# An S4 layer with a feed-forward block: eight of sixteen input rows get their shift after the move, four residual rows are loaded early, and the planned order is new

## The chip, the core and the metric

The kernel runs on one core of a Trainium2 chip. The metric is the device time of one execution in microseconds; the time of the kernel before is the median of three runs. The engines are named as in the profile: PE is TensorE's matmuls and PEld its weight loads, DVE is VectorE, ACT is ScalarE, POOL is GpSimd, SP issues most of the DMAs.

## What is computed

The input is 2048 tokens of 512 channels. A conditioning vector gives six vectors by a small product (`mod = silu(c) @ w_mod`). The first half is a layer norm with scale and shift, an S4 convolution over the tokens (by Fourier transforms of length 4096, its kernel K built from complex exponentials), a gate and a residual; the second half is a layer norm, a dense layer of 1792, a squared ReLU, a dense layer back, a gate and a residual.

```python
h = layernorm(x) * (1 + ca) + sa
K = einsum("dn,dnl,dn->dl", C, exp(dt * A * l), dt * B).real
y = irfft(rfft(h) * rfft(K)) + h * Dskip          # along the tokens
x = x + ga * y
h = layernorm(x) * (1 + cb) + sb
x = x + gb * (relu(h @ w1 + b1) ** 2 @ w2 + b2)
```

## The kernel before, in words

**Rows.** The input stands in memory as 16 blocks `xt[s]` of 128 x 512, the "rows". For each row the kernel takes mean and variance (L681, L682, with a power on GpSimd at L685 and L686, four rows at a time), subtracts the mean and multiplies by the gain `g1` (L729, VectorE, in place), and then moves the row into another layout with sixteen small matmuls on TensorE (L742). The matrix of the move, `sel`, is the identity scaled by the row's reciprocal deviation (L737, ScalarE). The shift `s4` of the modulation, the same for all rows, is put into the bank first, by a matmul of two constants (`pick`, `shift`, L739) into which the move accumulates. ScalarE copies the bank into `xj` (L745). The banks `ps` are three, shared by nearly everything before the feed-forward part.

**The S4 part.** Channels are worked in eight chunks. For chunk c, letters A to H are the transform of the input (stage 1 L789, stage 2 L799, copies on ScalarE L791 and L824), the digits 0 to 7 are the exchange of its halves by DMA (L834), letters a to h are the product with the kernel's transform (L949, VectorE) and the sums that go back (L957, copies L963). Stage 1 needs all sixteen rows. The kernel itself is made in 32 units u between these pieces: phases (L892, GpSimd), sines (L902 to L904, ScalarE), amplitudes (L914, L918, GpSimd), their products (L928 to L931, VectorE), a small matmul (L938) and its stage 1. The units need the parameters of their chunk (`parameters`, L595 to L664: the four first chunks at once, the other four as piece p, which itself is split over VectorE, ScalarE and GpSimd) and the exponentials (piece x, L883). Piece r is a row, l the later half of the modulation, w a part of the load of w1.

**What follows.** `inverse` (L1123) goes back to tokens, two row blocks at a time (L1131), and adds the residual `xt`: rows 0 to 3 on VectorE from a buffer `cd4` (L1140), the others on GpSimd (L1145). Then come layer norm, transposes (L1168) and the two dense layers in three float32r products per product (L1245, L1272 to L1274), which fill TensorE to the end.

**What sets the order.** `LOADS` is the order of the first loads on SP: x a row, p and P the two halves of the parameters, G, C and S three 1 MB blocks of `w_mod` (gate, scale, shift), t and e tables of the transforms, k Dskip. `ORDER` says which pieces are written between which units. That written order gives the dependencies and the ring of banks; then `keep_order` (L181) plans the sequence on each engine, with a cost for every instruction (`weight`, L121). `SPAN` is how far ahead a more urgent group may be taken before an earlier one, and `PASSES` how often the plan is made anew from its own latest starts. Matmuls in `in_turn` keep their written order; the inverse of rows 0 to 3 was among them. `paced_load` lets a load wait until the one before the last has landed. Engines work through their queues in order, so an instruction that waits holds all behind it.

## Time and profile before

| | |
|---|---|
| runs | 605.31 us median (601.77 to 606.57) |
| profiled execution | 605.23 us, of it 603.4 in the span |
| PE, PEld busy | 569.5, 494.1 us |
| DVE, ACT, POOL busy | 438.4, 421.5, 464.0 us |
| rows (first L739 to end of the last L745) | 24.6 to 49.5 us |
| stage 1 begins (L789) | 49.5 us |
| inverse begins (L1131) | 272.8 us |
| HBM read, written | 46.74, 4.19 MB |

Durations are those of one profiled execution. In a row of the timeline the first number is the start, the second the length (of a whole run of instructions where it ends in a count, x32); in brackets stands the idle time of that engine before it and what ended it. In a row of the groups stand the count, the busy time in us, the mean ns of one instruction, and the idle time before. The records of one fp32 matmul are two. "Issue" is time in which an engine waited for nothing that the profile shows.

### The profile page before, as it was taken

How to read it: one execution, taken by the hardware profiler on the slowest of the kernel's cores; microseconds unless marked ns; L12 is line 12 of the kernel's file. 1: busy time of each engine (PE TensorE's matmuls, PEld its weight loads, DVE VectorE, ACT ScalarE, POOL GpSimd, SP SyncE). 2: the span in 40 equal slices, each digit the busy share in tenths (PEclk: the TensorE clock that was granted, in tenths of full speed). 3: DMA queues.
4: the chain of work that ended last, by engine and by line, in shares of the span. 5: the costliest groups of instructions: out<-in, count | busy, mean ns of one | idle time of the engine just before them, and what ended most of it. 6: DMA issues, size and time to landing. Idle time of an engine off the chain costs nothing.

```text
span 603.4 us, 21634 instructions
## 1 busy us (share of the span) xinstructions
PE 569.5 (94%) x9396; PEld 494.1 (82%) x9396; DVE 438.4 (73%) x714; ACT 421.5 (70%) x788; POOL 464.0 (77%) x383
## 2 busy tenths in 40 slices
PE   1898999999999999998989999999999999998996
PEld 1667988999999998997778888888887888887885
DVE  7796688899798799746888945459859744547833
ACT  4997999998999879442879555546957555654440
POOL 5599999999999799160668998926689688892544
PEclk9999999999999999998999999999999999999999
DMA  8962033302130234274351332015354343201432
GB/s 306 398 193 72 5 73 74 64 12 44 34 74 4 51 104 100 52 195 145 103 147 57 105 104 89 22 45 176 107 153 127 112 119 102 70 18 35 158 88 86
DMA packets 45982, 60.70 MB, mean 101 GB/s; under 512 B 5184, under 2 KB 26816, under 8 KB 45760
## 3 DMA queue, kind: packets, MB, share of 16 engines
q1 hardware_dynamic: 45456, 59.20, 33.5%
q8 instruction: 73, 1.20, 0.9%
q10 hardware_dynamic: 432, 0.14, 0.1%
q14 instruction: 21, 0.17, 0.1%
HBM read 46.74 MB, written 4.19 MB: 84 GB/s over the span
## 4 chain that ended last, share of the span: by engine, by line
PE 69%; ACT 8%; POOL 7%; DVE 6%; issue 5%; DMA 4%; DVEq 0%; POOLq 0%; ACTq 0%; SPq 0%
PE ac L1245 9%; PE ps L1245 8%; PE ps L957 8%; PE ps L799 8%; PE ps L789 6%; PE ac L1274 4%; PE ac L1272 4%; PE ac L1273 4%; PE kg L938 4%; DMA xy<-w 4%; PE kg L1245 3%; PE ac L1131 3%; PE ps L1274 2%; PE ps L1272 2%; PE ps L1273 2%
## 5 line engine op out<-in xcount | busy, mean ns | idle before, releaser
L1214 POOL TENSOR_TENSOR w2r<-xy,w2r 128x512 fp32r<-128x512 f32 x56 | 80.1, 1431 | 53.9 <-ACT w2r L1213 53.7
L799 PE MATMUL ps<-xy,t_sb 128*64 128x64 f32 x2048 | 67.3, 223 | 1.0 <-issue 0.7
L799 PEld LDWEIGHTS ps<-xy,t_sb 128*64 128x64 f32 x2048 | 64.2, 138 | 3.1 <-issue 0.9
L957 PE MATMUL ps<-e_sb,xy 128*64 128x128 f32 (+2 forms) x1152 | 65.3, 267 | 1.1 <-issue 0.8
L957 PEld LDWEIGHTS ps<-e_sb,xy 128*64 128x64 f32 x1152 | 59.5, 140 | 2.6 <-issue 1.4
L1213 ACT CAST w2r<-xy 128x512 fp32r<-128x512 f32 x56 | 34.8, 624 | 27.1 <-PE ac L1274 12.7
L918 POOL TENSOR_TENSOR rtl<-tables 128x1024 f32<-128x1024 f32 x22 | 43.2, 1964 | 0.0
L1272 PE MATMUL ac<-w2r,r 128*128 128x512 f32 x110 | 42.8, 389 | 0.0
L1273 PE MATMUL ac<-w2r,r 128*128 128x512 f32 x110 | 42.8, 389 | 0.0
L1274 PE MATMUL ac<-w2r,r 128*128 128x512 f32 x110 | 42.8, 389 | 0.0
L791 ACT COPY xy<-ps 128x512 f32<-128x512 f32 x64 | 36.6, 590 | 8.7 <-PE ps L789 8.4
L1245 PE MATMUL ac<-tt,k1t 128*128 128x512 f32 x168 | 40.6, 390 | 1.5 <-DVE xy L1378 1.5
L949 DVE TENSOR_TENSOR xy<-ps,xy 128x512 f32<-128x512 f32 x64 | 40.1, 685 | 2.1 <-PE ps L799 1.1
L1245 PEld LDWEIGHTS ac<-tt,k1t 128*128 128x128 f32 x168 | 31.5, 188 | 8.4 <-DVE xy L1378 1.9
L1145 POOL TENSOR_TENSOR big<-big,xy 128x512 f32<-128x512 f32 x12 | 16.1, 1357 | 26.3 <-ACT big L1142 26.2
L1237 POOL TENSOR_TENSOR k1t<-xy,k1t 128x1024 fp32r<-128x1024 f32 x14 | 33.7, 2407 | 3.3 <-ACT k1t L1235 3.1
L892 POOL TENSOR_TENSOR rtl<-lo,big 128x1024 int32<-128x1024 int32 x16 | 34.3, 2143 | 2.4 <-ACT tg L904 2.3
L963 DVE COPY big<-ps 128x256 f32<-128x256 f32 (+1 forms) x66 | 24.7, 411 | 15.7 <-PE ps L957 15.5
L892 POOL TENSOR_TENSOR llph<-lo,big 128x1024 int32<-128x1024 int32 x16 | 34.5, 2157 | 0.8 <-ACT tg L904 0.8
L1272 PE MATMUL ps<-w2r,r 128*128 128x512 f32 (+1 forms) x88 | 34.7, 394 | 0.0
L789 PE MATMUL ps<-d_sb,big 128*64 128x128 f32 x512 | 32.1, 274 | 2.4 <-ACT xy L791 1.7
L1274 PE MATMUL ps<-w2r,r 128*128 128x512 f32 (+1 forms) x88 | 34.0, 386 | 0.0
(297 smaller groups left out, 1693.8 us busy)
## 6 DMA issues: line engine op xcount, KB each, us to landing
xy<-w SPq DMA_DIRECT2D x91, 256.0 KB, 2.8
xy<-xt SPq DMA_DIRECT2D x32, 256.0 KB, 4.5
xy<-xy SPq DMA_DIRECT2D x32, 256.0 KB, 3.6
xy<-w_mod SPq DMA_DIRECT2D x6, 1024.0 KB, 9.0
out_dram<-p SPq DMA_DIRECT2D x15, 256.0 KB, 2.0
t_sb<-c_t SPq DMA_DIRECT2D x1, 2048.0 KB, 11.5
i2c<-c_i SPq DMA_DIRECT2D x4, 512.0 KB, 4.2
big<-prm SPq DMA_DIRECT2D x2, 768.0 KB, 6.2
```

What stands on the lines that cost most here:

```text
L789: nc.tensor.matmul(ps[64 * r : 64 * r + 64, 128 * i : 128 * i + 128], src[:, i], d1_sb[:, r], start=True, stop=True)
L791: copy(dst[:, o // 4], ps.rearrange("p (t m) -> p m t", t=4))
L799: nc.tensor.matmul(ps[64 * r : 64 * r + 64, 64 * i : 64 * i + 64].rearrange("p (h q t) -> p q h t", h=2, t=2), t2_sb[:, 8 * g + i, r], src ...
L892: nc.gpsimd.tensor_tensor(ph.rearrange("p d r (a b) -> p (d r) a b", a=4), bc(low_phase[:, us].rearrange("p d r b -> p (d r) b"), 2, 4), b ...
L918: nc.gpsimd.tensor_mul(am[:, 0, :, 32:96].rearrange("p d (v x) -> p d v x", v=2), bc(et[:, 256 + 8 * d0 : 384 + 8 * d0].rearrange("p (y a) ...
L949: nc.vector.tensor_mul(product_piece(y, g), ps, piece(x, g))
L957: nc.tensor.matmul(ps[64 * m : 64 * m + 64], pairs(y)[:, g, i // 2, 64 * m : 64 * m + 64, i % 2], e1_sb[:, h].rearrange("p (r j) -> p r j" ...
L1214: nc.gpsimd.tensor_sub(to[:, 1], wst, to[:, 0].bitcast(F32))
L1245: nc.tensor.matmul(ps[:, cols], x, y, start=(i == 0 and not onto), stop=(i == 5), skip_group_check=onto)
L1272: pe.append(nc.tensor.matmul(bank_, r2l[:, ms], hi_[:, cols], start=(f == begin), stop=False))
L1273: pe.append(nc.tensor.matmul(bank_, r2h[:, ms], lo_[:, cols], start=False, stop=False))
L1274: pe.append(nc.tensor.matmul(bank_, r2h[:, ms], hi_[:, cols], start=False, stop=(f == end_)))
```

## The change

*The shift of a row.* A string `EVAC` gives each row a way out of its bank. Rows with a (4 to 8, 10, 13, 14) are as before. For v (2, 3, 11, 12, 15) the matmul of `pick` and `shift` is left out, and VectorE adds `s4` as it takes the bank over. For g (0, 1, 9) it is left out too, ScalarE copies the bank, and GpSimd then adds `s4` in place.

*The residual's first rows.* A new piece y, as soon as the last amplitude has been issued, loads xt[0] to xt[3] into four parts of `p1`, which lies where the second exponential table was; before, they went into a spectrum buffer together with rows 4 to 7, behind the table of the inverse. The inverse of rows 0 to 3 is no longer in `in_turn`.

*Order.* `LOADS`, `ORDER`, `PASSES` and `SPAN` are new, and the planner's cost knows a transpose. The line numbers of the changed kernel are larger: L739 is L744, L742 is L747, L745 is L754 (the adds are L752 and L756), L729 is L732, L892 is L904, L1131 is L1152.

```diff
+EVAC = "ggvvaaaaagavvaav"
-LOADS = "pxxxxxxxxGCSxxxxxxxkPtxe"
+LOADS = "xxxxpxGxxCPxSxxxxketxxxx"
-PASSES, SPAN = 7, 400
+PASSES, SPAN = 10, 150
-    "rrrrrrrrrrxxrrrrrrBCCBpACCBCBAABCCBAB.AAAAC..lB.0aaaa1.a.Daa.x.DabbbbDEDEE.b.2Ebb.bD.DcDccccEDc.E.Fc"
+    "rrrrrrrrrrrrrrrrBCBCCBAAAxCBABABCCxC..ApAABC.l0.aaBaa1..aDaaD..abbbbEDEEbbE.E.b.D.Db2DDcxccDc3..EcEc"
...
+            if ins.is_transpose:
+                return 88, 88 + 130
...
-            nc.tensor.matmul(ps.rearrange("p (g d) -> p g d", g=4), pick, bc(shift, 1, 4), start=True, stop=False)
+            late = EVAC[s] != "a"
+            if not late:
+                nc.tensor.matmul(ps.rearrange("p (g d) -> p g d", g=4), pick, bc(shift, 1, 4), start=True, stop=False)
             for g in range(4):
                 for q in range(4):
                     nc.tensor.matmul(
                         ps[32 * q : 32 * q + 32, 128 * g : 128 * g + 128], sel[:, g // 2, 32 * (g % 2) : 32 * (g % 2) + 32],
-                        row[:, 128 * q : 128 * q + 128], start=False, stop=(g == 3))
-            moved.append(nc.scalar.copy(xj[:, :, 4 * s : 4 * s + 4], ps.rearrange("p (g d) -> p d g", g=4)))
+                        row[:, 128 * q : 128 * q + 128], start=late, stop=late or g == 3)
+            to, of = xj[:, :, 4 * s : 4 * s + 4], ps.rearrange("p (g d) -> p d g", g=4)
+            if EVAC[s] == "v":
+                nc.vector.tensor_add(to, of, bc(s4, 2, 4))
+            else:
+                nc.scalar.copy(to, of)
+            if EVAC[s] == "g":
+                nc.gpsimd.tensor_add(to, to, bc(s4, 2, 4))
+            moved.append(s)
...
+    def early_rows():
+        assert amped[-1] == NU - 1
+        late.append(held(kp, "k01", "p1", [P, 7, 512]))
+        for s in range(4):
+            paced_load(late[0][:, 3 + s], xt[s])
+        yield
...
-    xts = [cs_[s] if s < 4 else ds_[s % 4] for s in range(16)]
-    for s in range(8):
+    xts = [ds_[s % 4] for s in range(16)]
+    for s in range(4, 8):
         paced_load(xts[s], xt[s])
...
-    cd4 = runs(spectra[3]).rearrange("p (s q c d) -> p s q c d", s=4, q=4, c=NC)
+    cd4 = p1[:, 3:7].rearrange("p s (q c d) -> p s q c d", q=4, c=NC)
...
-        if s0 < 4:
-            in_turn.update(whole)
```

How the plan moves instructions is seen at three places. First, ScalarE's queue at the start of the rows, before: `tables` are the exponentials, `tg0` the angle of the first parameters, `big1` the moved rows.

```order
L635 ACT_TABLE_LOAD
L635 ACTIVATE tg0_171<-halfpi_70 128x1
L636 ACTIVATE tg0_171<-tg0_171 128x256
L719 CAST shift_319<-s4_318 128x128
L883 ACT_TABLE_LOAD
L883 ACTIVATE tables1_338<-big0_86 128x2x64 x16
L745 COPY big1_87<-ps1_163 128x128x4
```

And now:

```order
L639 ACTIVATE tg0_171<-tg0_171 128x256
L740 ACTIVATE big0_86<-ident_66,mv1_74 128x2x64
L895 ACT_TABLE_LOAD
L895 ACTIVATE tables0_337<-big0_86 128x64 x8
L648 ACT_TABLE_LOAD
L648 ACTIVATE big0_86<-big0_86 128x4x64
L649 ACTIVATE big0_86<-big0_86 128x4x64
L650 ACTIVATE big0_86<-big0_86,halfpi_70 128x4x64
L722 CAST shift_319<-s4_318 128x128
L895 ACT_TABLE_LOAD
L895 ACTIVATE tables1_338<-big0_86 128x2x64 x8
L754 COPY big1_87<-ps1_163 128x128x4
```

The sine of the first parameters (L648 to L650), with a table load of its own, has come ahead of the first copy of a row; a batch of exponentials has gone behind the arctangent (L639), and eight of the wide ones behind the first copies.

Second, VectorE's queue at the same place, before; `ps0` holds the product that becomes `s4`, `xy0` are rows 0 to 3, `xy2` rows 8 to 11:

```order
L681 BN_STATS st1_76<-xy2_96 128x6
L715 TENSOR_TENSOR s4_318<-ps0_162,gs4_316 128x128
L681 BN_STATS st2_77<-xy2_96 128x6
L720 SCALAR_TENSOR_TENSOR shift_319<-shift_319,small_71,s4_318 128x128
L681 BN_STATS st3_78<-xy2_96 128x6
L682 BN_AGGR mv1_74<-st0_75 128x2
L682 BN_AGGR mv1_74<-st1_76 128x2
L729 SCALAR_TENSOR_TENSOR xy0_94<-xy0_94,mv1_74,kg0_320 128x512 x4
```

And now:

```order
L642 SCALAR_TENSOR_TENSOR tg0_171<-tg0_171,big0_86 128x256
L643 SCALAR_TENSOR_TENSOR tg0_171<-tg0_171,big0_86 128x256
L644 SCALAR_TENSOR_TENSOR tg0_171<-tg0_171,big0_86 128x256
L645 TENSOR_SCALAR big0_86<-tg0_171 128x4x64
L732 SCALAR_TENSOR_TENSOR xy0_94<-xy0_94,mv1_74,kg0_320 128x512 x3
L684 BN_STATS st0_75<-xy2_96 128x6
L718 TENSOR_TENSOR s4_318<-ps0_162,gs4_316 128x128
```

Four steps of the angle stand ahead of the first rows, and `s4` is read behind three rows instead of ahead of all.

Third, SP's queue near the end of the S4 part, before:

```order
L1318 DMA lo_341<-b2 128x512
L669 DMA xy0_94<-xy4_98 64x1024 x4
L669 DMA raw1_3665<-w1 128x4x128
L669 DMA i2c_4586<-c_i2 128x1024 x4
L669 DMA xy4_98<-xt 128x512 x4
L669 DMA xy0_94<-xt 128x512 x4
```

And now:

```order
L1337 DMA lo_341<-b2 128x512
L672 DMA xy6_100<-xy2_96 64x1024 x4
L672 DMA raw1_3803<-w1 128x4x128
L672 DMA p1_4562<-xt 128x512 x4
L672 DMA i2c_4586<-c_i2 128x1024 x4
L672 DMA xy3_97<-xt 128x512 x4
```

Four loads of the residual have moved from behind the inverse's table `i2c` to ahead of it, into `p1`.

More of the change, by code (lines that the diff above doesn't have):

```diff
@@ L44 @@
 EXP_PART = 8
-PASSES, SPAN = 7, 400
+PASSES, SPAN = 10, 150
 EXPS = [(0, 1), (1, 1), (2, 2), (4, 2), (6, 2)]
 ORDER = (
-    "rrrrrrrrrrxxrrrrrrBCCBpACCBCBAABCCBAB.AAAAC..lB.0aaaa1.a.Daa.x.DabbbbDEDEE.b.2Ebb.bD.DcDccccEDc.E.Fc"
-    "3EFc.E.ddddGd.Fd.GxFd4.F.dGeeeeF..FGGFHeGeGe5..wHeffGHfff.w.f.H.HffH6ggHgw.g.g.H.g7ghhhghw"
+    "rrrrrrrrrrrrrrrrBCBCCBAAAxCBABABCCxC..ApAABC.l0.aaBaa1..aDaaD..abbbbEDEEbbE.E.b.D.Db2DDcxccDc3..EcEc"
+    "..cEFcFdFdddGdGFd..FdF..4GdeeGee..xFFeGe.e.5GGHeffHGfffHwf.H.f..Hw6fHHggHgg....gggw7hhhhwyg"
 ).split(".")
@@ L1032, in load_pieces @@
             yield
-    work["w"] = load_pieces()
+    late = []
+    def early_rows():
[4 more added lines that the diff above has]
+        yield
+    work["w"], work["y"] = load_pieces(), early_rows()
     next(work["x"])
@@ L1094, in tile_adaln_ssm_ffn @@
     w2r = held(kp, "k00", "w2r", [P, 3, 2, 512], FR)
-    p1 = held(kp, "k01", "p1", [P, 7, 512])
+    p1 = late[0]
     for _ in last:
```

## The prediction

> **What bounds the kernel now.** I read the page first, then busy time by stage, then the timeline of the first 60 us, where the change sits.
>
> ```profile
> PE 569.5 (94%) x9396; PEld 494.1 (82%) x9396; DVE 438.4 (73%) x714; ACT 421.5 (70%) x788; POOL 464.0 (77%) x383
> ```
>
> TensorE is busy for 569.5 of 603.4 us, so 34 us of idle is all that ordering can win; work taken off TensorE comes on top. By stage:
>
> ```profile
> 0.00:50.00 50.00, 33.57 (x648) 24.47 (x650) 41.26 (x109) 40.01 (x133) 35.74 (x58) 1.00 0.76 271
> ...
> 49.00:267.00 218.00, 211.97 (x6122) 201.68 (x6122) 179.43 (x294) 188.96 (x293) 197.29 (x144) 1.00 0.26 61
> ...
> 100.00:160.00 60.00, 59.51 (x1684) 56.98 (x1682) 51.09 (x85) 55.56 (x92) 59.53 (x45) 1.00 0.18 39
> ...
> 270.00:275.00 5.00, 3.84 (x147) 3.36 (x143) 1.38 (x4) 0.00 (x0) 0.00 (x0) 1.00 0.46 147
> 275.00:280.00 5.00, 4.65 (x171) 3.88 (x175) 3.48 (x11) 0.85 (x3) 0.00 (x0) 0.70 0.48 151
> ...
> 320.00:603.00 283.00, 276.93 (x1240) 228.63 (x1238) 179.34 (x217) 161.19 (x279) 209.83 (x167) 1.00 0.31 94
> ```
>
> The columns are the length, then PE, PEld, DVE, ACT and POOL busy, the granted clock, the DMA share and GB/s. Half of all idle, 16.4 us, lies ahead of 50 us. From 49 to 267 us TensorE idles 6.0 us, and GpSimd beside it is as full (59.53 of 60 from 100 to 160 us): a stage with two bounds. From 320 us on TensorE runs matmuls that the change does not touch; I cost that stage at nothing. The row stage itself:
>
> ```profile
> 24.61 0.50 PE L739 MATMUL ps<-shift,pick 128*128 128x512 f32 x1 [0.29 <-DVE shift L720]
> ...
> 26.08 1.08 PE L742 MATMUL ps<-xy,big 128*32 128x128 f32 x32 [0.98 <-DVE xy L729]
> ...
> 28.53 0.51 PE L739 MATMUL ps<-shift,pick 128*128 128x512 f32 x1
> ...
> 28.96 1.08 PE L742 MATMUL ps<-xy,big 128*32 128x128 f32 x32
> ...
> 29.97 0.50 PE L739 MATMUL ps<-shift,pick 128*128 128x512 f32 x1
> ```
>
> A row takes 29.97 - 28.53 = 1.44 us of TensorE, of which the shift's matmul takes 28.96 - 28.53 = 0.43 and the move 1.01. Thirteen rows from 29.97 give 48.7, and so it ends:
>
> ```profile
> 48.87 0.59 ACT L745 COPY big<-ps 128x512 f32<-128x512 f32 x1 [0.85 <-PE ps L742]
> ...
> 49.51 2.84 PE L789 MATMUL ps<-d_sb,big 128*64 128x128 f32 x48 [0.70 <-ACT big L745]
> ```
>
> From row 3 on, TensorE alone sets the pace of this stage.
>
> **The change part by part.** Removed: eight shift matmuls, 8 x 0.43 = 3.4 us of TensorE. That is a gain only if nothing else in the row stage ends later, so I follow each queue. The rows for it:
>
> ```profile
> 17.77 1.28 ACT L737 ACTIVATE big<-ident,mv 128x128 f32<-128x128 f32 x4 [0.51 <-POOL mv L686]
> ...
> 17.58 1.94 PE L698 MATMUL ps<-xy,srep 128*32 128x128 f32 x32 [0.68 <-DMA xy<-w_mod]
> ...
> 18.96 1.32 ACT L883 ACTIVATE tables<-big 128x64 f32<-128x64 f32 x8
> ...
> 20.38 1.93 PE L698 MATMUL ps<-xy,srep 128*32 128x128 f32 x32 [0.86 <-DMA xy<-w_mod]
> ...
> 22.09 1.28 ACT L635 ACT_TABLE_LOAD   x1
> ...
> 23.60 0.37 ACT L636 ACTIVATE tg<-tg 128x256 f32<-128x256 f32 x1
> ...
> 23.88 0.29 ACT L719 CAST shift<-s 128x128 fp32r<-128x128 f32 x1
> ...
> 25.22 3.35 DVE L729 SCALAR_TENSOR_TENSOR xy<-xy,mv,kg 128x512 f32<-128x512 f32 x5
> 25.48 3.96 ACT L883 ACTIVATE tables<-big 128x128 f32<-128x128 f32 x16
> ...
> 29.24 1.11 ACT L745 COPY big<-ps 128x512 f32<-128x512 f32 x2
> ...
> 31.25 0.43 DVE L639 SCALAR_TENSOR_TENSOR tg<-tg,big 128x256 f32<-128x256 f32 x1
> ...
> 38.59 0.50 ACT L647 ACTIVATE big<-big,halfpi 128x256 f32<-128x256 f32 x1
> ```
>
> *Start on VectorE.* The first L729 ran at 25.22. Now four steps of the angle (0.43 each, L639 to L642 of before) stand ahead of it and wait for ScalarE's arctangent. ScalarE has one batch of eight exponentials (1.32) less ahead of that, and 0.6 of new waiting, so it falls near 22.8 instead of 23.60, and the first three rows are ready at about 25 to 26.8: no gain. Behind them stand one BN_STATS (0.69) and the read of the shift s4 out of bank ps0, which ends at 27.8; row 2 needs that bank. The S load, moved behind two row loads and the second half of the parameters, lands later than the 20.38 above: 0.75 MB more go ahead of it, where the 1 MB matrices land 20.38 - 17.58 = 2.8 us apart, so some 2 us; VectorE is later still, so this costs nothing. The last four rows land behind the 2 MB table t2, all loads together as late as before; VectorE comes to their BN_STATS at 38 or later, so that is covered too, and would cost its own lateness one for one if VectorE were quick.
>
> *ScalarE.* Behind the arctangent (over at 23.2) now stand one row's scaling (1.28 / 4 = 0.3), a table load (1.28), eight exponentials (1.32), a table load for the sine (1.28), three sine steps (some 0.45 each, 1.3), the shift's cast (0.29), a third table load (1.28) and eight wide exponentials (half of 3.96). Only then comes the copy of row 0: 23.2 + 9.0 = 32.2, where before it was 29.24. All this work was there before, but the sine came in the middle of the rows. Row 3 needs the bank that this copy frees: 32.9, where before it was 30.40. Row 3 and the twelve behind it take eight times 1.44 and five times 1.01, 16.6 us, so TensorE is done at 49.5 at best, 0.8 later than before: what the removed matmuls give is used up by the late start.
>
> *VectorE to the end of the rows.* The moved shift reads PSUM and writes 128x512, as L949 does; on GpSimd it reads SBUF, as L1145 does:
>
> ```profile
> L949 DVE TENSOR_TENSOR xy<-ps,xy 128x512 f32<-128x512 f32 x64 | 40.1, 685 | 2.1 <-PE ps L799 1.1
> ...
> L1145 POOL TENSOR_TENSOR big<-big,xy 128x512 f32<-128x512 f32 x12 | 16.1, 1357 | 26.3 <-ACT big L1142 26.2
> ...
> L681 DVE BATCH_NORM_STATS2 st<-xy 128x6 f32<-128x512 f32 x16 | 10.6, 685 | 0.9 <-DMA xy<-xt 0.9
> ...
> L931 DVE TENSOR_TENSOR rtl<-rtl,tg 128x1024 f32<-128x1024 f32 x22 | 26.8, 1216 | 0.0
> ```
>
> From 27.8 its queue holds, up to the last of its five shifts: 7 BN_STATS (4.8), 13 L729 (8.7), five shifts (3.4), five products of the first kernel units (two at 1.22, three at 0.69: 4.5), and some 3.6 of small steps (eight aggregations, four integer shifts, the shift's sign; the sizes are estimates from the same stretch of the timeline). That is 25.0 with no wait, so row 15 is shifted at 52.8. Its bounds: 50 if a third of the small steps overlap, 55 with waits. ScalarE loses five copies of 0.59; nobody waits for that.
>
> *GpSimd.* Its three shifts are 3 x 1.36 = 4.1 us.
>
> ```profile
> 28.16 0.73 POOL L592 TENSOR_TENSOR big<-big 128x256 f32<-128x256 f32 x1 [5.52 <-DMA big<-prm]
> ...
> 48.97 2.13 POOL L892 TENSOR_TENSOR rtl<-lo,big 128x1024 int32<-128x1024 int32 x1
> ...
> L914 POOL TENSOR_TENSOR rtl<-tables 128x512 f32<-128x512 f32 x22 | 23.5, 1072 | 0.8 <-PE kg L938 0.8
> ```
>
> The second half of the parameters is now loaded ahead of the S matrix, which removes most of the 5.52 us wait, and two of its products are put off. By its queue the first phase (L892) starts near 40.6 instead of 48.97, 8.4 earlier. Behind it then stand the two put-off products (1.5), a table product (1.1), the last two powers (1.3), a fix of the tables (0.6) and the shifts (4.1): 8.6. Its pace after that is as before, and its shifts end near 53, as VectorE's do. So the first stage-1 matmul starts at 52.8 instead of 49.51: **+3.3**. One kernel unit's matmuls, 1.05 us, are done ahead of it, which leaves **+2.2**.
>
> *49 to 267 us.* Here the order is new throughout, the instructions are the same. Two kernel units are ready when stage 1 begins, where before TensorE came to the first one after fourteen other groups of stages 1 and 2. A lead like that can close gaps; GpSimd's unchanged pace keeps it from growing. Of the 6.0 us idle I take half, **-3.0**; the bounds are -6.0 (none left) and +4.1 (GpSimd's added work in full).
>
> *The residual's first rows and the inverse.* The inverse is L1131, and the place is quoted above with its clock. From the timeline:
>
> ```profile
> 270.20 14.42 SPq L669 DMA_DIRECT2D xy<-xt  x8
> ...
> 275.35 1.07 PE L1131 MATMUL ac<-big,i2c 32*32 32x128 f32 x65 [1.50 <-issue]
> ```
>
> TensorE stops for 1.5 us on nothing but its own issue, while eight row loads fill the queues; then comes a stretch whose clock is 0.70 over 5 us, another 1.5. The trace does not tell what the stop waits for. Four of the eight loads now go ahead of it, into the last kernel buffer, and of the last product two more groups stand between the two pairs of the inverse. The stop may stay or go: half of 3.0, **-1.5**, bounds -3.0 and 0. On SP's queue the four early loads stand ahead of the table of the inverse (i2c). They wait for GpSimd's last amplitude, and then for quiet queues:
>
> ```profile
> 245.00:250.00 5.00, 5.00 (x174) 4.84 (x172) 4.96 (x8) 1.70 (x4) 0.00 (x0) 1.00 0.02 3
> ```
>
> GpSimd is done by then, and the loads' share is 0.02, so they cost nothing; should they go out late, the inverse waits for four loads more, at 14.42 / 8 = 1.8 us each 7.2. That the inverse's first four rows lose their fixed turn on TensorE adds no instruction and takes none away: nothing.
>
> Sum: 2.2 - 3.0 - 1.5 = -2.3. The profiled execution took 605.23 us (603.4 of it the span), and the median of the runs is 605.31, so the two stand for the same; 605.2 - 2.3 = 602.9.
>
> *A rule against this change.* After the stop the clock fell. It does so at a second place:
>
> ```profile
> 310.00:315.00 5.00, 3.29 (x116) 2.52 (x102) 4.67 (x17) 3.52 (x13) 3.80 (x4) 0.95 0.42 134
> 315.00:320.00 5.00, 5.00 (x21) 4.21 (x21) 4.00 (x8) 3.73 (x10) 1.28 (x2) 0.71 0.50 150
> ...
> L717 PE MATMUL kg<-g,ident 128*128 128x128 f32 x8 | 2.1, 441 | 0.0
> ...
> L1069 PE MATMUL ps<-gb,ident 128*128 128x128 f32 x8 | 1.2, 288 | 0.0
> ```
>
> 1.7 us of idle are followed by a clock of 0.71, some 1.5 us lost. The last two rows are the groups by line: early in the kernel one form of matmul takes 441 ns that later takes 288, although the clock's record says 1.00 there, so the start is slow as well. In the changed order rows 0 to 3 are thin, four moves of 1.08 us in the 7 us from 25.9, and the low clock may last into the rows behind them. I count nothing for it, since rows 0 to 3 wait for ScalarE anyway; where that cover is gone it is 1.5 us for each such stretch. The Trainium skill, "TensorE: Matmul & The Clock Gate" (part 1, what is actually happening), says that an idle window of some 3.4 us sets the clock to half until a busy one has passed. By that rule the stops agree, and two stretches here would be slow.
>
> **The rivals.** *The queues do not hold the rows.* If VectorE and ScalarE run ahead of my sums, the 3.4 us come off whole: -3.4 - 3.0 - 1.5 = -7.9, 597.3. For it: VectorE's steps overlap in the timeline, and the sum of its queue has bounds of 50 and 55. Against it: three table loads stand in ScalarE's queue, and their time is sure.
>
> *GpSimd becomes the bound*, the slower case. Its 4.1 us of shifts push every later kernel unit back, while TensorE, with less of its own work ahead of each unit, needs it some 3 us sooner, and waits at the units' matmuls (L938). The first stage-1 matmul at 54 (+4.5, less 1.05, is +3.4), +4.1 up to 267 us, nothing gained at the inverse: +7.5, 612.7. It decides from a first phase later than about 44. For it: 59.53 of 60 us busy. Against it: before, TensorE idles 6 us in 218, and none of its long waits is for GpSimd.
>
> *Half clock in the row stage*, two stretches of it uncovered: 602.9 + 3.0 = 605.9.
>
> *The change does not do what it says*: the late rows take all that the order gives, 605.2.
>
> **How the numbers follow.** Forecast 0.52, the faster rival 0.26, GpSimd 0.11, half clock 0.05, nothing 0.06. About 1%, 6 us, is what a measurement of this kernel can tell from no change. The forecast's own bounds, 599.5 to 607, lie within that, as do the last two, so faster 0.26, same 0.63, slower 0.11. The range 596 to 609.5 takes in the row stage's bounds and the centre of the faster rival; left out are that rival's far side and the GpSimd case.
>
> **What would show it.** Right: the first stage-1 matmul near 52.8 and the copy of row 0 near 32; the first phase near 41; about 3 us idle on TensorE from 49 to 267 us; no stop of 1.5 us in the inverse. A first stage-1 matmul at 47 or earlier shows the faster rival, TensorE waiting at the units' matmuls the slower one. The prediction is wrong if the idle from 49 to 267 us moves by more than 4, or the stage from 320 us on by more than 2.

## The result and the profile after

The changed kernel takes 607.35 us (median of 20 executions) where the kernel before takes 604.1: a ratio of 1.0052, 95% interval 1.0032 to 1.0072, so 3.1 us slower (0.0052 x 603.4, the mean of the four medians that the kernel before had, the one here and the three beside the runs below). Forecast were 602.9 us beside 605.2, a gain of 2.3. The time lies in the range, the sign is wrong.

The page of the changed kernel and its busy time by stage (columns as before: length, PE, PEld, DVE, ACT, POOL, clock, DMA share, GB/s):

```profile
PE 568.5 (94%) x9388; PEld 493.3 (81%) x9388; DVE 442.1 (73%) x719; ACT 417.9 (69%) x783; POOL 463.0 (76%) x386
```

```profile
30.00:40.00 10.00, 8.49 (x165) 5.79 (x165) 10.00 (x22) 8.87 (x33) 9.84 (x10) 0.83 0.92 279
...
49.00:267.00 218.00, 213.57 (x6190) 202.57 (x6181) 184.99 (x301) 185.15 (x298) 193.80 (x145) 1.00 0.27 63
...
320.00:603.00 283.00, 275.73 (x1225) 226.55 (x1223) 175.62 (x221) 158.31 (x278) 205.11 (x166) 0.99 0.31 92
```

TensorE's instructions are eight shift matmuls fewer, and from 49 to 267 us it idles 218 - 213.57 = 4.4 us instead of 6.0. The surprise lies in the stretch of the last row. Its timeline, with the first and the last second-layer matmul and every wait of TensorE over 0.25 us between them:

```profile
316.70 0.39 PE L1291 MATMUL ac<-w2r,r 128*128 128x512 f32 x1
...
333.72 1.66 PE L1264 MATMUL kg<-tt,k1t 128*128 128x512 f32 x6 [0.53 <-DVE xy L1397]
...
459.78 0.73 PE L1264 MATMUL ac<-h1h,k1t 128*128 128x512 f32 x2 [1.73 <-DVE r L1276]
...
548.44 2.93 PE L1264 MATMUL ac<-tt,k1t 128*128 128x512 f32 x6 [2.67 <-DVE xy L1397]
...
600.54 0.28 PE L1293 MATMUL ps<-w2r,r 128*128 128x256 f32 x1
```

The same in the kernel before:

```profile
320.15 0.39 PE L1272 MATMUL ac<-w2r,r 128*128 128x512 f32 x1
...
460.66 0.72 PE L1245 MATMUL ac<-h1h,k1t 128*128 128x512 f32 x2 [0.42 <-DVE r L1257]
...
548.16 1.65 PE L1245 MATMUL ac<-tt,k1t 128*128 128x512 f32 x6 [1.51 <-DVE xy L1378]
...
598.59 0.28 PE L1274 MATMUL ps<-w2r,r 128*128 128x256 f32 x1
```

The changed kernel comes to this point 320.15 - 316.70 = 3.45 us sooner, and then takes 600.54 + 0.28 - 316.70 = 284.12 us for matmuls that the kernel before does, in the same order on TensorE, in 598.59 + 0.28 - 320.15 = 278.72. I call this stretch the feed-forward part; it lost 5.4 us. What stood ahead of the longest wait, on VectorE and GpSimd of the changed kernel:

```profile
537.59 5.10 POOL L1391 TENSOR_TENSOR big<-big,lo 128x512 f32<-128x512 f32 x4
537.64 0.69 DVE L1400 TENSOR_TENSOR xy<-ac,p 128x512 f32<-128x512 f32 x1 [1.43 <-PE ac L1264]
...
541.54 4.22 DVE L1424 TENSOR_TENSOR r<-rs,r 128x512 fp32r<-128x512 f32 x1 [2.42 <-ACT r L1423]
542.65 1.29 POOL L1233 TENSOR_TENSOR w2r<-xy,w2r 128x512 fp32r<-128x512 f32 x1
543.91 1.30 POOL L1391 TENSOR_TENSOR big<-big,lo 128x512 f32<-128x512 f32 x1
545.68 0.75 DVE L1406 SCALAR_TENSOR_TENSOR ac<-ac,b1c,p 128x512 f32<-128x512 f32 x1
...
547.70 0.68 DVE L1397 TENSOR_TENSOR xy<-ac,p 128x512 f32<-128x512 f32 x1
```

A subtraction of 128x512 (L1424, the low half of a squared tile that is needed much later) lies on VectorE for 4.22 us, as long as GpSimd works without a pause (to 545.2 us), and behind it in the queue stand the four instructions of which the last (L1397) is what TensorE waits for. In the kernel before the same subtraction is L1405:

```profile
543.28 3.37 DVE L1405 TENSOR_TENSOR r<-rs,r 128x512 fp32r<-128x512 f32 x1
```

It took 3.37 us, but one of those four (L1406, there L1387) stood ahead of it and another (L1275, there L1256) behind the addition that TensorE waits for.

So the theory (A): the rows' part gives the 2 to 3 us that I forecast, and the feed-forward part loses 5 because the new plan put VectorE's instructions there in another order, in which subtractions that GpSimd holds up stand in front of what TensorE needs. Its rivals: what the rows' part gains is given back later whatever the order (B); the subtraction waits for something other than GpSimd; or the loss is spread over the whole reordered part, and no single place carries it.

### The profile page after: what moved, and what is told of

Read it like the earlier page. It is cut to its first block, busy times and chain, and to the rows that moved or that the text cites. A ratio compares the mean times of both kernels' runs of the same rounds, so it can differ in the third digit from the quotient of the medians.

```text
span 605.4 us, 21642 instructions
## 1 busy us (share of the span) xinstructions
PE 568.5 (94%) x9388; PEld 493.3 (81%) x9388; DVE 442.1 (73%) x719; ACT 417.9 (69%) x783; POOL 463.0 (76%) x386
## 4 chain that ended last, share of the span: by engine, by line
PE 69%; ACT 10%; DVE 9%; POOL 7%; issue 4%; DMA 0%; ACTq 0%; DVEq 0%; POOLq 0%
PE ac L1264 9%; PE ps L811 7%; PE ps L969 7%; PE ps L1264 6%; PE ps L801 5%; PE ac L1291 4%; PE ac L1292 4%; PE ac L1293 4%; PE ps L1291 3%; PE ps L1293 3%; PE ps L1292 3%; PE kg L950 3%; PE kg L1264 3%; PE ac L1152 2%; ACT tg L914 2%
## 5 line engine op out<-in xcount | busy, mean ns | idle before, releaser
L1264 PE MATMUL ac<-tt,k1t 128*128 128x512 f32 x168 | 41.9, 399 | 2.7 <-DVE xy L1397 2.7
L1264 PEld LDWEIGHTS ac<-tt,k1t 128*128 128x128 f32 x168 | 32.2, 193 | 9.8 <-DVE xy L1397 3.1
L1256 POOL TENSOR_TENSOR k1t<-xy,k1t 128x1024 fp32r<-128x1024 f32 x14 | 34.7, 2482 | 3.7 <-ACT k1t L1254 3.7
L904 POOL TENSOR_TENSOR rtl<-lo,big 128x1024 int32<-128x1024 int32 x16 | 34.4, 2149 | 2.3 <-ACT tg L916 1.6
L904 POOL TENSOR_TENSOR llph<-lo,big 128x1024 int32<-128x1024 int32 x16 | 34.6, 2160 | 1.5 <-ACT tg L916 1.5
L1291 PE MATMUL ps<-w2r,r 128*128 128x512 f32 (+1 forms) x88 | 34.8, 396 | 0.0
L1293 PE MATMUL ps<-w2r,r 128*128 128x512 f32 (+1 forms) x88 | 34.0, 386 | 0.0
L1292 PE MATMUL ps<-w2r,r 128*128 128x512 f32 (+1 forms) x88 | 33.9, 385 | 0.0
```

What stands on the lines that cost most here:

```text
L904: nc.gpsimd.tensor_tensor(ph.rearrange("p d r (a b) -> p (d r) a b", a=4), bc(low_phase[:, us].rearrange("p d r b -> p (d r) b"), 2, 4), b ...
L1264: nc.tensor.matmul(ps[:, cols], x, y, start=(i == 0 and not onto), stop=(i == 5), skip_group_check=onto)
L1291: pe.append(nc.tensor.matmul(bank_, r2l[:, ms], hi_[:, cols], start=(f == begin), stop=False))
L1292: pe.append(nc.tensor.matmul(bank_, r2h[:, ms], lo_[:, cols], start=False, stop=False))
L1293: pe.append(nc.tensor.matmul(bank_, r2h[:, ms], hi_[:, cols], start=False, stop=(f == end_)))
```

## The experiments

Each kernel's total is a ratio to the kernel before on the same chip. The length of the feed-forward part is read from its trace by the same two instructions as above; what is left of the difference lies ahead of it. "Ahead" is the ratio's difference times 603.4 us less the feed-forward part's, all in us; by the intervals it is good to about 1 to 2 us, and kernels with the same queues in that part (changed, e1, e3, e4, e9, e11) stand from -0.3 to -2.7 in it.

| kernel | ratio (95%) | total | feed-forward | against before | ahead |
|---|---|---|---|---|---|
| before | 1 | | 278.72 | | |
| changed | 1.0052 (1.0032 to 1.0072) | +3.1 | 284.12 | +5.4 | -2.3 |
| e1 new front, old queues behind | 1.0071 (1.0047 to 1.0096) | +4.3 | 285.72 | +7.0 | -2.7 |
| e2 old front, new queues behind | 1.0136 (1.0098 to 1.0175) | +8.2 | 286.31 | +7.6 | +0.6 |
| e3 a quarter of the b2 adds | 0.9996 (0.9971 to 1.0021) | -0.2 | 279.71 | +1.0 | -1.2 |
| e4 three subtractions later | 0.9951 (0.9929 to 0.9973) | -3.0 | 278.43 | -0.3 | -2.7 |
| e9 the third alone | 0.9992 (0.9966 to 1.0018) | -0.5 | 280.53 | +1.8 | -2.3 |
| e11 five moves | 0.9989 (0.9972 to 1.0006) | -0.7 | 278.34 | -0.4 | -0.3 |
| e7 before, one later | 0.9994 (0.9972 to 1.0016) | -0.4 | 277.80 | -0.9 | +0.5 |
| e6 e4, rows loaded late | 0.9965 (0.9937 to 0.9994) | -2.1 | 279.36 | +0.6 | -2.7 |
| e5 e4, all shifts by matmul | 1.0217 (1.0182 to 1.0252) | +13.1 | 280.62 | +1.9 | +11.2 |
| e8 planner's numbers undone | 1.0098 (1.0064 to 1.0133) | +5.9 | 278.84 | +0.1 | +5.8 |
| e10 before with eight shifts | 1.0158 (1.0139 to 1.0177) | +9.5 | 278.99 | +0.3 | +9.2 |

### Three instructions later (e4), and the third alone (e9)

In e4 nothing but VectorE's queue is touched, by a key behind the plan, after which each engine takes its groups in the order of the keys. The numbers are groups of the plan: 2404 is the subtraction L1424 shown above, 2353 the addition L1397.

```diff
     last = {}
+    key = dict(zip(sequence, range(len(sequence))))
+    for g, h in ((1431, 1532), (1972, 2038), (2404, 2353)):
+        key[g] = key[h] + 0.5
...
     for g in sequence:
```

> The changed kernel with three instructions of VectorE's queue put later, and nothing else moved on any engine: the subtraction that ends at 333 us goes behind the addition for which the matmuls of line 1264 waited 0.53 us, the one at 453 us goes behind the pair of subtractions that the matmuls waited 1.73 us for, and the one at 541 us goes behind the addition that they waited 2.67 us for. Theory A (these three stand in front of what the matmuls need): the three waits fall below 0.3, 0.5 and 0.5 us, the half clock behind the third goes, and the time falls by 4 to 5 us to about 602.5, a ratio of 0.997 to before. Rival (the loss is spread over the whole reordered part, or the waits only change their place): under 1.5 us gained, a ratio of 1.003 or more.

The median was 600.9 us beside 603.64 of the kernel before, 0.9951 (0.9929 to 0.9973): by the intervals faster than both kernels. By the ratios it gained 6.1 us on the changed kernel, more than the 4 to 5 expected. In its trace (all lines are 14 higher; L1438 is the subtraction, L1411 the addition):

```profile
314.64 0.39 PE L1305 MATMUL ac<-w2r,r 128*128 128x512 f32 x1
...
339.17 4.25 PE L1278 MATMUL ps<-tt,k1t 128*128 128x512 f32 x17 [0.82 <-POOL k1t L1270]
...
541.01 0.69 DVE L1411 TENSOR_TENSOR xy<-ac,p 128x512 f32<-128x512 f32 x1
541.62 0.69 DVE L1438 TENSOR_TENSOR r<-rs,r 128x512 fp32r<-128x512 f32 x1
...
592.79 0.28 PE L1307 MATMUL ps<-w2r,r 128*128 128x256 f32 x1
```

The three waits are gone; the one of 0.82 us is new, and the only one over 0.25 that is left. The subtraction takes 0.69 us. The feed-forward part is as long as before, 278.43 us. The other two are subtractions of 128x1024, also with both inputs in the on-chip buffer. In the changed kernel the second was this row:

```profile
453.20 3.42 DVE L1207 TENSOR_TENSOR tt<-rawh,tt 128x1024 fp32r<-128x1024 f32 x1
```

In e4 it took 1.22 us, at 456.08; the first took 2.31 us at 330.75 in the changed kernel. The loss of the changed kernel is thus in the place of three of the plan's 719 VectorE instructions; the rival that spreads it over the reordered part falls.

> The changed kernel with only the third of e4's instructions later: the subtraction at 541 us behind the additions. It prices one wait. In the changed kernel this place has a wait of 2.67 us, and the six matmuls behind it take 2.93 us instead of 1.65. Theory A: both go, 1.5 to 3.9 us together (the lower end since the kernel before, with its 1.51 us there and no slow matmuls behind it, gained nothing that could be measured in e7), so 603.4 to 605.8 beside 603.3 of before, with the most likely value 604. Rival (the three waits of the changed kernel lie in a row, and what one gains the next takes): no change, 607.

With `((2404, 2353),)` alone the median was 602.69 us beside 602.92. The feed-forward part is 284.12 - 280.53 = 3.6 us shorter than in the changed kernel, within the 1.5 to 3.9 us expected and near the 2.67 of the wait and the 2.93 - 1.65 = 1.28 by which the six matmuls behind it had been slow. One instruction made the difference between a loss and no loss; the other two are worth 280.53 - 278.43 = 2.1 us.

### Less work for GpSimd, the same order (e3)

```diff
-                behind.append((anchor, nc.gpsimd.tensor_add(x2[:, s], x2[:, s], d4(b2g)).ins))
+                part = lambda t: t[:, 0:1]
+                behind.append((anchor, nc.gpsimd.tensor_add(part(x2[:, s]), part(x2[:, s]), part(d4(b2g))).ins))
```

> The changed kernel with every queue in its own order, but each of the 16 GpSimd additions of the second layer's bias to a row of the residual takes 128x128 of its 128x512 elements: three quarters of that addition are left out. Theory A with the blocked port (a VectorE subtraction with both inputs in the on-chip buffer can't run while GpSimd works back to back): the subtraction of line 1424 at 541.5 us takes about 0.7 us instead of 4.22, the matmuls' wait of 2.67 us at 548 falls under 0.5, with it the half clock behind it, and the total falls by 3 to 4 us, to about 603.5. The other two losses, at 333 and 459 us, stay, since other GpSimd work lies there. Rival (the subtraction waits for its ScalarE copy or a buffer, not for GpSimd): it ends as late as before and the time moves by under 0.5 us.

602.67 us beside 603.64. The place in its trace (L1567 is the subtraction, L1375 and L1534 are GpSimd's work, L1406 the product):

```profile
539.20 1.29 POOL L1375 TENSOR_TENSOR w2r<-xy,w2r 128x512 fp32r<-128x512 f32 x1 [2.21 <-ACT w2r L1374]
539.68 1.37 DVE L1567 TENSOR_TENSOR r<-rs,r 128x512 fp32r<-128x512 f32 x1 [2.42 <-ACT r L1566]
540.45 0.92 POOL L1534 TENSOR_TENSOR big<-big,lo 128x128 f32<-128x128 f32 x1
...
541.02 4.36 PE L1406 MATMUL ac<-tt,k1t 128*128 128x512 f32 x18
```

No queue is changed, but now GpSimd pauses for 2.21 us ahead of the subtraction, which takes 1.37 us instead of 4.22 (0.7 was expected), and the 18 matmuls go through with no wait. The waits at 332 and 458 us stay (0.43 and 1.64 us), as expected. So it is GpSimd that holds the subtraction up. The Trainium skill, "SBUF — State Buffer" (who interferes with whom), says that a VectorE instruction with two inputs in that buffer contends with a GpSimd instruction that reads it, over a port pair that one of them takes whole, and that one with at most one such input, outside the two-port modes, does not. The trace of the changed kernel agrees: L1400, with one input in a bank, took its 0.69 us at 537.64 beside the same work of GpSimd that held the subtraction for 4.22 us.

### The two halves exchanged (e1, e2)

The plan's last 1070 groups, from the pair loop on (the loop over the two halves of the dense layers), are the same in both kernels. In e1 the changed kernel takes them in the order of the kernel before (`TAIL`, their starts in that plan); in e2 it is the other way round.

```diff
+    tail = len(groups) - len(TAIL)
+    start = min(begin[g] for g in range(tail, len(groups)) if of[g][0] == "PE")
+    key = begin[:tail] + [start + t for t in TAIL]
```

> The changed kernel up to the pair loop; from there on (the last 1070 groups of the plan) every engine takes its instructions in the order in which the kernel before takes them. Theory A (the rows' part gains about 3.4 us and the new order of VectorE, ScalarE and GpSimd in the feed-forward part loses about 5.4): the first second-layer matmul stays near 316.5 us and the stage from there to the end is that of before again, so 600.7 us where before has 604.1, a ratio of 0.994. Theory B (what the rows' part gains is lost later through what it left behind, loads and buffers, whatever the order): near 607, a ratio of 1.005. Theory C (neither, the difference is one of the chip's states): a ratio of 1.000.

> The mirror image: the kernel before up to the pair loop, and from there on the order of the changed kernel on every engine. Theory A: the first second-layer matmul near 319.9 us and some 5 us lost behind it, so 609 us, a ratio of 1.009. Theory B: as before, a ratio of 1.000. If the two parts don't add (the new order fits the new start and loses only 2 us here, or more than 7), the loss belongs to the meeting of both and to neither alone.

e1 took 607.08 us, e2 610.15, both beside 603.64. Theory A had 600.7 for e1 and is wrong there; 607 is what B had named. The front keeps its gain (-2.7), but the old order behind it loses 7.0 us, more than the new one. Where, in e1:

```profile
316.55 1.71 POOL L1341 TENSOR_TENSOR xy<-xy 128x256 f32<-128x256 f32 x1 [2.44 <-DMA xy<-w]
...
321.47 1.05 ACT L1345 CAST k1t<-xy 128x1024 fp32r<-128x1024 f32 x1 [1.56 <-POOL xy L1344]
...
322.81 1.03 ACT L1297 CAST tt<-rawh 128x1024 fp32r<-128x1024 f32 x1
...
323.87 2.92 DVE L1298 TENSOR_TENSOR tt<-rawh,tt 128x1024 fp32r<-128x1024 f32 x1 [3.81 <-ACT tt L1297]
...
328.10 1.22 PE L1355 MATMUL ps<-h0h,k1t 128*128 128x512 f32 x2 [3.75 <-DVE r L1367]
...
331.68 0.63 PE L1384 MATMUL ac<-w2r,r 128*128 128x512 f32 x1
```

From top to bottom: GpSimd waits for a load of w1, ScalarE's copy L1345 waits for GpSimd's sums and holds the copy L1297 behind it, VectorE waits 3.81 us for that copy, and TensorE 3.75 us for VectorE. With the old front TensorE comes to this stretch later (320.15 us for the first second-layer matmul, 314.68 in e1), and the chain has time. After the wait the matmuls take 0.63 us instead of 0.40, up to 333.4 us.

e2, in turn, has waits at the three places of the changed kernel (1.08, 1.97 and 2.65 us) and one more of 0.82 us; another, of 1.43 us at 318.97, lies just ahead of the stretch.

```profile
338.59 1.64 PE L1336 MATMUL kg<-tt,k1t 128*128 128x512 f32 x6 [1.08 <-DVE xy L1469]
...
346.78 4.15 PE L1336 MATMUL ps<-tt,k1t 128*128 128x512 f32 x17 [0.82 <-POOL k1t L1328]
...
465.60 0.74 PE L1336 MATMUL ac<-h1h,k1t 128*128 128x512 f32 x2 [1.97 <-DVE r L1348]
...
554.27 2.93 PE L1336 MATMUL ac<-tt,k1t 128*128 128x512 f32 x6 [2.65 <-DVE xy L1469]
```

So the new order loses behind 320 us with the old front too (7.6 us here, in the trace of an execution of 613.87 us where the median is 610.15), and B, which had e2 as fast as before, does not hold. But the two halves do not add. The old order behind the new front loses 7.0 us, at another place, in a chain that begins at a load, as B supposed; and by e2's expectation a loss of more than 7 us there belongs to the meeting of front and order, not to the order alone. The old order is no remedy, because it fits only the old front. The remedy is the new order with three places mended.

### One instruction later in the kernel before (e7)

Group 2401 (L1405) goes behind 2350 (L1378), with the same key as in e4.

> The kernel before with a single instruction of VectorE's queue put two places later: the subtraction of line 1405 that took 3.37 us at 543.28 goes behind the additions of lines 1390 and 1378, for the second of which the matmuls of line 1245 waited 1.51 us at 548.16. Theory A (a subtraction held up by GpSimd in front of what the matmuls need): the wait falls to 0.5 us or less and the time by 1.0 to 1.6 us, a ratio of 0.998 to before. Rival (the matmuls would wait for the addition anyway): no change, 1.000.

602.14 us beside 602.8, a ratio of 0.9994: no change that can be told. The wait itself went; the place (L1419 is the subtraction, L1404 and L1392 are the additions):

```profile
542.71 2.57 POOL L1386 TENSOR_TENSOR big<-big,lo 128x512 f32<-128x512 f32 x2
543.17 0.75 DVE L1404 SCALAR_TENSOR_TENSOR saved<-ac,b1c,xy 128x512 f32<-128x512 f32 x1 [0.60 <-PE ac L1259]
544.52 0.69 DVE L1392 TENSOR_TENSOR xy<-ac,p 128x512 f32<-128x512 f32 x1 [0.61 <-PE ac L1259]
545.13 0.70 DVE L1419 TENSOR_TENSOR r<-rs,r 128x512 fp32r<-128x512 f32 x1
```

L1404 and L1392 read a bank (`ac`) and one tile each, and take 0.75 and 0.69 us in the middle of GpSimd's 2.57; the subtraction with both inputs in the on-chip buffer follows as GpSimd ends, at 545.28. The feed-forward part came out 0.9 us shorter, not 1.5, since the wait near 460 us was 1.38 us in this trace and 0.42 in that of before. (With the old order that wait was 0.28 to 1.38 us in five traces, with the new one 1.61 to 1.97 in the four that leave its subtraction in place.) A gain of 0.9 us lies inside the interval (0.9972 to 1.0016), so the expectation of a ratio of 0.998 is neither met nor refuted.

### What the front's gain is made of (e5, e6, e8, e10)

Four kernels undo or isolate a part. e5 and e6 have e4's order behind the pair loop and e10 that of the kernel before; in all four the queues ahead of it are planned anew.

```diff
e5  -EVAC = "ggvvaaaaagavvaav"
    +EVAC = "aaaaaaaaaaaaaaaa"
e6  -    p1 = late[0]
    +    p1 = held(kp, "k01", "p1", [P, 7, 512])
    -    for s in range(4, 8):
    +    for s in range(8):
             paced_load(xts[s], xt[s])
e8  -PASSES, SPAN = 10, 150
    +PASSES, SPAN = 7, 400
    -            if ins.is_transpose:
    -                return 88, 88 + 130
e10 (in the kernel before)
    +EVAC = "ggvvaaaaagavvaav"
```

> The changed kernel with the three VectorE instructions later, as in e4, and with all 16 rows shifted by the matmul and moved by ScalarE again, as in the kernel before; the order of pieces, the early loads and the queues from the pair loop on stay those of e4. e4 took 600.9 us beside 603.6 of before. Theory A1 (the gain ahead of the pair loop comes from the order of the pieces and from shorter waits between 49 and 267 us, and the eight shifts behind the move matter little, since the shift's matmuls lie in a stage where TensorE waits for row 0's copy and for tables anyway): within 1 us of e4, 600.5 to 602. Theory A2 (taking eight shifts off TensorE is the gain): 3 us or more are lost, 604 or more. The first matmul of the first stage, at 51.2 us in the changed kernel, tells where: A1 leaves it within 1 us.

> The kernel of e4 with the first four rows of the residual loaded where the kernel before loads them, into a quarter of the spectrum, after the last product; the rest as in e4. If the early load is what starts the inverse sooner, the first matmul of the inverse and the first second-layer matmul come 1 to 2 us later than in e4, and the time is 602 to 603. If the inverse waits for instruction fetches and for the first statistics anyway, the time is within 0.7 us of e4, 600.2 to 601.6.

> The changed kernel with the planner's numbers of the kernel before: 7 passes, a span of 400 and no separate weight for transposes. From the pair loop on this gives VectorE, SyncE and TensorE the order of before, and ScalarE and GpSimd almost (15 and 4 places differ). If the numbers are what costs the time behind the pair loop, 601 us. If, as e1 says, the old order does not fit the earlier start either (a wait of 3.75 us near 328 us for the low half of a squared tile), 606 to 608, with that wait in the trace again.

> The kernel before with one edit, the same eight rows shifted behind the move on VectorE or GpSimd; pieces, loads, planner's numbers and the order from the pair loop on are those of before. e5 showed that the new order of pieces without these shifts costs 15 us. Theory 1 (the eight shifts are a gain of their own, by the matmuls and the waits for shift vectors that they take off TensorE): 1 us or more faster than before, 602 or less. Theory 2 (the gain is only in the two together, because the new order moves rows before their shift is there): within 1 us of before or slower, since VectorE and GpSimd are busy in this stage with the tables' work and the first stage starts no sooner: 603 to 608.

e5 took 616.33 us, e6 600.74 and e8 607.93, beside 602.8; e10 took 612.94 beside 602.92. For e5 theory A2 holds, by far more than its 3 us: the eight shifts matter, and the first stage moved by 5.6 us. e5's trace shows the shift's matmul in the way again:

```profile
28.36 0.80 PE L837 MATMUL ps<-shift,pick 128*128 128x512 f32 x1 [3.84 <-DVE shift L816]
...
56.77 3.71 PE L894 MATMUL ps<-d_sb,big 128*64 128x128 f32 x64 [1.79 <-ACT big L847]
```

TensorE waits 3.84 us for the shift vector ahead of the first row, and its first stage starts at 56.77 us instead of 51.19. That gives half of the 11.2 us; most of the rest is a wait between 80 and 150 us for the copy of a kernel unit, in the waits of that stretch (us in total, times, longest):

```profile
PE ps L894 <- DVE ksb L1124: 5.3, 1, 5.3
```

In e10 the eight shifts, put into the old order, start the first stage later too:

```profile
52.22 7.21 PE L890 MATMUL ps<-d_sb,big 128*64 128x128 f32 x128 [0.91 <-DVE big L841]
```

at 52.22 us against 49.51 in the kernel before. By the inverse it is 8.4 us behind (281.20 against 272.79), with no single wait of TensorE over 1.6 us between; what spreads the loss there is not shown. That is theory 2, at a price beyond its range. So neither the shifts nor the order of the pieces is worth anything alone: each without the other costs 9 to 11 us ahead of the feed-forward part, and the two with the planner's numbers, which e8 takes away, gain some 2 (0.3 to 2.7 in the six rows of the table with this front). Each of these kernels was planned anew, so they price the parts together with the plan that came of them, not a matmul by itself.

e6 is within the noise of e4 (0.9965 against 0.9951): loading four residual rows early is worth nothing that can be measured, though the intervals leave room for some 2 us either way. In its trace the inverse starts at 274.14 us (270.11 in e4), but that execution was the longest of its twelve (606.33 us, the median 600.74), so only the total is used here. In e8 the feed-forward part is that of before again (278.84 us), which puts the new order there down to the planner's numbers; the gain ahead of it went with them (its first stage starts at 54.31 us, 4.8 later than in the kernel before). So its time came as e1 suggested (606 to 608), but for another reason: the wait near 328 us is not in its trace, since its front is later.

### Two more moves (e11)

```diff
-    for g, h in ((1431, 1532), (1972, 2038), (2404, 2353)):
+    for g, h in ((1431, 1514), (1520, 1514), (1972, 2038), (2404, 2353), (1512, 1529)):
```

> The kernel of e4 with two more moves near 330 us, for the wait of 0.82 us on GpSimd at 339 that is left there: on VectorE an addition of the first layer goes ahead of two subtractions of 1.65 and 1.75 us (ScalarE waited 5.4 us for it), and on GpSimd the sums' low halves go ahead of a low half of the second layer's weights. If nothing else takes the place of that wait, 0.5 to 1 us less than e4, 600 us; if the sums wait for their loads or for ScalarE anyway, the same as e4, 600.9 beside 603.6 of before, a ratio of 0.995.

601.72 us beside 602.92. The wait of 0.82 us became two of 0.28 and 0.34 in its trace, and the feed-forward part is 0.1 us shorter than e4's. The total, 0.9989, is not below e4's 0.9951, and neither of the two expected times came. The queues up to the pair loop are the same in both, and yet all of the difference lies there, so two such totals can part by 2 us without a cause in the queues. e4 has the lowest ratio here, but how much it gains on the kernel before is known no better than that.

## Why the prediction was right or wrong

*The row stage, +2.2: right in its mechanism, a little too dear.* These are the rows of the changed kernel that answer to its steps:

```profile
30.81 0.64 ACT L754 COPY big<-ps 128x512 f32<-128x512 f32 x1
...
37.94 2.14 POOL L904 TENSOR_TENSOR rtl<-lo,big 128x1024 int32<-128x1024 int32 x1
...
45.91 3.25 POOL L756 TENSOR_TENSOR big<-big,s 128x512 f32<-128x512 f32 x3
...
49.88 1.12 PE L950 MATMUL kg<-rtl 128*32 128x64 f32 x64
50.25 0.68 DVE L752 TENSOR_TENSOR big<-ps,s 128x512 f32<-128x512 f32 x1
...
51.19 3.71 PE L801 MATMUL ps<-d_sb,big 128*64 128x128 f32 x64 [0.19 <-POOL rtl L930]
```

The first copy of a row came at 30.8 us (32.2 forecast), the first phase at 37.9 (40.6), the end of VectorE's last shift at 50.9 (52.8), that of GpSimd's at 49.2 (53), and the first stage at 51.19 (52.8), with one unit's matmuls ahead of it as forecast. So the stage cost 1.7 - 1.1 = 0.6 us, not 2.2. The sums of the queues were up to 4 us too long; GpSimd's shifts took 3.25 / 3 = 1.08 us each, not the 1.36 of the residual's add.

*49 to 267 us, -3.0:* 1.6 us less idle in this trace, 2.5 and 2.4 in those of e3 and e4. Right in direction, but smaller; that half of the idle would go was a choice, not a sum.

*The inverse, -1.5: the size came, but by luck.* The first inverse matmul came at 271.3 us instead of 272.8, and the first second-layer matmul 3.45 us sooner, so about 1.9 us were won between them. But the stop on "issue" is still there, and so is the slow clock behind it (0.68 from 280 to 285 us):

```profile
280.82 1.98 PE L969 MATMUL ps<-e_sb,xy 128*64 128x96 f32 x31 [1.90 <-issue]
```

From the first inverse matmul to the first matmul of the first dense layer it took 287.94 - 271.25 = 16.7 us, and 289.57 - 272.79 = 16.8 in the kernel before. The 1.9 us were won behind that: the kernel before has a stop of 1.71 us at 313.63 and then the clock of 0.71 that the prediction quotes, the changed kernel one of 1.12 us at 312.68 and a clock of 1.00. I had counted nothing for that second place. That the early loads bring any of it is not shown, since e6 does as well without them.

*The sum ahead of 320 us, -2.3:* -2.3 by the ratio, -3.45 in the one trace. Of the rivals, the half clock came for one stretch (0.83 in the row of 30 to 40 us above, 1.00 there before), behind this wait:

```profile
31.50 1.08 PE L747 MATMUL ps<-xy,big 128*32 128x128 f32 x32 [2.86 <-ACT big L754]
```

The two rows from 32.52 us took 36.88 - 32.52 = 4.36 us of TensorE instead of 2 x 1.44. That is 1.5 us, and the wait for ScalarE, which the prediction had taken for its cover, was over by then. What covered it is VectorE's queue, whose last shift ended 0.26 us ahead of the first stage. GpSimd did not become the bound of the kernel units: from 49 to 267 us no wait of TensorE for it was over 0.2 us.

*From 320 us on, nothing: this is the step that failed.* I wrote that TensorE there "runs matmuls that the change does not touch". That is true of TensorE, whose order there did not change, and it is not enough. `PASSES`, `SPAN` and the transposes' cost plan the whole program, and in the last 1070 groups they gave 71 of VectorE's 207 places and 102 of ScalarE's 272 to other instructions. The order was followed at three places, all ahead of this stage, so the price of nothing had no reading of these queues behind it. The stage cost +5.4 us: the three waits of TensorE 0.53, 1.73 - 0.42 and 2.67 - 1.51, in sum 3.0; slower matmuls behind the third, 1.28; and 1.1 in smaller steps. Matmul by matmul the two traces part at five places only: 0.8 us at 333.72, 0.4 at 343.66, 1.3 at 459.78, 2.5 from 548.44 on and 0.3 at 559.65. What the runs showed in place of the nothing: subtractions on VectorE, held up by GpSimd, stand in front of what TensorE needs, and putting three of them later takes 5.7 us off this stage (e4), the third alone 3.6 (e9). No rival of the prediction had that either. The prediction named more than 2 us in this stage as what would make it wrong, and that is what happened. That the kernel before had a wait of 1.51 us for VectorE at 548 us stood in its trace, and was the warning.

## What to carry to other kernels

When a change touches a planner's numbers, it touches every stage that the planner orders: compare each engine's queue over the whole program, and read the places where the busiest engine already waits, not only those where the edit was made. On VectorE, put an instruction with both inputs in the on-chip buffer behind the ones that TensorE needs whenever GpSimd is busy without pause beside it: one such instruction cost 3.6 us here, though in the kernel before the like move (e7) gained nothing that can be told. And parts that were tuned together can't be priced alone: each half of this change by itself cost 9 to 11 us, where the whole gained some 2 ahead of 320 us.

## What the runs showed of the hardware

A VectorE subtraction of 128x512 with both inputs in the on-chip buffer took 0.69 and 0.70 us as GpSimd's work ended (e4, e7), and 3.37 and 4.22 us beside it (the kernel before, the changed one). In the changed kernel it began at 541.54 us, and GpSimd went from one instruction to the next at 542.65 and at 543.91 without letting it in; it ended 0.55 us after GpSimd's row of instructions was over. In e3 it did get in: of its 1.37 us the last 0.69 begin at 540.36, where one instruction of GpSimd ended (540.49) and the next, back to back, took 0.92 where its like took 0.49. The Trainium skill, "SBUF — State Buffer" (who interferes with whom), speaks of a lock held for one whole instruction; here the hold-up lasted through three instructions of GpSimd, and what decides whether a waiting VectorE gets in between two is open.

TensorE's waits have a second price. Clock by windows (the last but two column), in the changed kernel around its wait of 2.67 us, then in e1 behind its wait of 3.75:

```profile
545.00:548.00 3.00, 0.76 (x4) 0.30 (x2) 2.99 (x5) 1.50 (x3) 0.21 (x1) 1.00 0.30 82
548.00:552.00 4.00, 3.56 (x10) 2.85 (x11) 1.58 (x3) 0.88 (x2) 0.00 (x0) 0.57 0.00 0
```

```profile
330.00:336.00 6.00, 6.00 (x20) 4.83 (x19) 3.44 (x3) 1.86 (x4) 5.51 (x6) 0.69 0.47 132
```

The wait of 1.51 us in the kernel before was followed by six matmuls in 1.65 us; that of 2.67 by the same six in 2.93, and that of 3.75 by more than 5 us of matmuls at 0.63 instead of 0.40 us. The Trainium skill, "TensorE: Matmul & The Clock Gate" (part 1, what is actually happening), gives a window of some 3.4 us that runs freely, and an idle one as what halves the clock. The measurement decides: a wait of 2.67 us was enough here. The prediction said that its two stops agree with that rule; they were 1.50 and 1.71 us, so as to length they do not. Nor does the length of a wait alone decide: those two and one of 1.90 us (at 280.82, changed kernel) were followed by clocks of 0.70, 0.71 and 0.68 over 5 us, but the matmuls behind 1.51 us (548.16, before), 1.73 us (459.78, changed kernel) and 1.97 us (465.60, e2) ran at full speed.

The trace of one execution is sharp in one stage and blurred in another. With the same queues up to the pair loop, the first second-layer matmul fell at 316.7, 315.1, 314.6, 317.4 and 315.9 us (changed kernel, e3, e4, e9, e11; the last two ran on another chip than e3 and e4), a spread of 2.7 us, while the feed-forward part of three kernels with the old order, or nearly so (before, e8, e10), was 278.7, 278.8 and 279.0 us long.
